# New constants in the planner that orders the work of a linear-attention and MoE kernel

## The chip, the cores and the metric

One core of one Trainium2 chip. The metric is the device time of one execution in microseconds; the number quoted is the median of three executions.

## The reference

Two parts, one after the other (cut to what is computed):

```python
mag = np.sqrt(a_re * a_re + a_im * a_im)
scale = np.minimum(mag, 0.999) / (mag + 1e-06)
ar, ai = a_re * scale, a_im * scale              # B=4, H=8, S=768, D=48
for t in range(S):
    new_re = ar[t] * S_re - ai[t] * S_im         # the state: D x D for each (b, h)
    new_im = ar[t] * S_im + ai[t] * S_re
    S_re, S_im = new_re + k[t] v[t]^T, new_im
    y[t] = q[t] @ S_re
x = y reordered to 3072 tokens x 384
h = x @ w_in                                     # 384 -> 2048
out = (gelu_erf(h)) @ w_out                      # 2048 -> 384
```

The weights arrive as float64 words; the result is float32.

## The kernel before, in words

The kernel has four kinds of work, and each step of each kind carries its kind's name.

- **lanes0 to lanes3** (`ticks`, `tick`, L1091, L703): the running products of the decays, on 128 partitions, in 24 slices of 8 rows over four groups of the sequence. For a slice s: `normalise` (part a: squares, `Ln`/`Exp` on ACT, multiplications of tiles `a` and `tab`), `scan` (part s: for each row one DVE product `tt` and one DVE sum `bt`), `towards` and `against` (part b: products into `xt`, then DMAs of `xt` to DRAM `kq`). `ending` (part e) closes a group.
- **weights** (`weights`, w0 to w15, each an "in" and an "out" piece): the float64 words of a piece are loaded into `raw`, ACT squares them for a range flag, four DVE steps build `wh` and the low half (`wi_lo`/`wo_lo`), ACT copies the high half (`wi_hi`/`wo_hi`), three PE products with `ident_r` and `minus` sum what the high half left over, and a copy (ACT or DVE) stores it as low half.
- **units** (`unit`, u0 to u23, 128 tokens each): loads `kqn` and `vn`, turns them (by PE transposes up to u7, by DVE transposes from u8), scores `qT,kp`, the state `st` with its gain (`m`), and the output, split into `xT` high (ACT) and `xT` low (DVE).
- **blocks** (`block`, j0 to j8, 2 or 3 units each): for each of 16 slices f of the hidden width, `first(f)` multiplies `xT` with `wi_hi`/`wi_lo` into `ph`; ACT writes `gh` and `gf` (Gelu), DVE `gl` = `gf` − `gh`; `second(f)` multiplies `gh` with `wo_hi` and `wo_lo`, and `gl` with `wo_hi`, into `po`. The units of the next block are written between the slices f of this one.

None of this is issued in the order of the code. `Plan` records every call as a step with its engine (or several engines that could run it, `either` and `both`), its cost from a table of constants, and what it depends on. `natural` (L274) gives each step a rank: the longest path to the end, plus an offset for the step's kind, `MORE`. The vector steps of the lanes are a chain of their own: along it each step counts with `WL` times its cost. `forward` (L292) plays the program through with a model of the queues; at every moment an engine takes the ready step with the highest rank, and a step that several engines can run goes where its modelled end plus `BIAS` of that engine is smallest. `backward` takes the ranks anew from the result; after four such passes (`PASSES`) the shortest modelled order is kept and issued (`issue`, L420 ff., hence all instructions carry L429). On the chip each engine, and SP's DMA queue, runs its instructions strictly in that order.

The few lines that use the three constants:

```python
if s.chain is not None:
    if s.chain in nextof:
        t = max(t, rest[nextof[s.chain]] + cost * s.weight)
...
return [t + MORE[s.kind] for t, s in zip(rest, steps)]
...
ends = {o: max(free[o], ready[i], ...) + c + BIAS[o] for o, (_, c) in steps[i].options.items()}
if ends[e] > min(ends.values()) + 1e-9:
    ...
...
P.chain["vector"] = "lanes", WL
```

Of the kernel before, what the change touches and what calls it, by code (L numbers as in the profile page):

```python
# [94 lines left out]
EARLIER, N_RAW, N_KP = 1, 4, 2  # L95
PASSES = 4
N_A = 4
WL = 4.532

MORE = dict(lanes0=483.83, lanes1=-1595.06, lanes2=-3639.85, lanes3=-3453.18, weights=-1624.01, units=-66.21, blocks=-85.66)  # L100
BIAS = dict(vector=-0.82, scalar=-1.94, gpsimd=0.93, sync=-6.23)


class Step:
# [8 lines left out]
class Plan:  # L113
# [160 lines left out]
    def natural(self):  # L274
# [4 lines left out]
        for i in range(len(steps) - 1, -1, -1):  # L279
# [9 lines left out]
            rest[i] = t  # L289
        return [t + MORE[s.kind] for t, s in zip(rest, steps)]  # L290

    def forward(self, rank):  # L292
# [14 lines left out]
        while len(order) < len(steps):  # L307
            best = None
            for e, waiting in pool.items():
# [8 lines left out]
                if len(steps[i].options) > 1:  # L318
                    ends = {o: max(free[o], ready[i], port[other[o]] if o in steps[i].port else 0.0) + c + BIAS[o] for o, (_, c) in steps[i].options.items()}
                    if ends[e] > min(ends.values()) + 1e-9:  # L320
# [119 lines left out]
def lanes_and_chunks(ctx, tc, flags, a_lanes, x_lanes, v_units, w_in, w_out, out):  # L440
# [650 lines left out]
    def ticks(g):  # L1091
        P.chain["vector"] = "lanes", WL
        with P.work(f"lanes{g}"):
            for s in range(end):
                if slices[s][0] == g:
                    tick(s)
        P.chain.pop("vector")
# [255 lines left out]
```

## Time and profile before

| | us |
|---|---|
| executions | 660.78, 662.86, 663.88 |
| median | 662.86 |
| span of the profiled execution, first to last instruction | 659.6 |
| median less that span | 3.3 |
| PE busy (share of the span) | 614.1 (93%) |
| DVE busy | 484.1 (73%) |
| ACT busy | 434.1 (66%) |
| POOL busy | 26.1 (4%) |

The profile is of one execution and gives its span only; times of single steps are times of that execution. PE is TensorE, PEld its weight loads, DVE VectorE, ACT ScalarE, POOL GpSimd, SP the queue of the DMAs. Names such as `gl<-gf,gh` are the tile written and the tiles read, as the program names them. A row of a timeline begins with the start in us from the start of the span and the duration.

### The profile page before, as it was taken

The numbers are of one execution on the slowest core, as the hardware profiler recorded it, in microseconds if no ns is written. First come the engines' busy times: TensorE is split into PE (matmuls) and PEld (weight loads), VectorE is DVE, ScalarE is ACT, GpSimd is POOL, SyncE is SP. The second block draws the span as 40 slices with busy tenths as digits, with TensorE's granted clock in tenths as the row PEclk, the third lists the DMA queues.
The fourth block names the chain that finished last, engine by engine and source line by source line (L and its number), as shares of the span: only waits on it lengthen the run. The fifth ranks groups of instructions, "written<-read, shape, count | busy, mean of one in ns | idle before, by whom it ended". The sixth has DMA issues, their size and how long they took to land.

```text
span 659.6 us, 13997 instructions
## 1 busy us (share of the span) xinstructions
PE 614.1 (93%) x5154; PEld 563.8 (85%) x5154; DVE 484.1 (73%) x1204; ACT 434.1 (66%) x1107; POOL 26.1 (4%) x74
## 2 busy tenths in 40 slices
PE   4655499999999999999999999999999999999995
PEld 2322277988789999999999999999999999999995
DVE  6999999999999999999989999656334424232211
ACT  8976699999998979787476997535442422232332
POOL 1000100002000000120000000020000000000000
PEclk9787699999999999999999999999999999999999
DMA  9366876668266456687889966487444132110000
GB/s 322 119 158 161 256 225 212 185 196 258 71 197 173 116 135 177 163 173 158 198 198 219 230 157 166 116 167 169 104 88 88 50 64 46 34 51 15 25 1 27
DMA packets 210442, 93.51 MB, mean 142 GB/s; under 512 B 167744, under 2 KB 202688, under 8 KB 210368
## 3 DMA queue, kind: packets, MB, share of 16 engines
q1 hardware_dynamic: 210368, 92.57, 54.6%
q8 instruction: 41, 0.67, 0.4%
q14 instruction: 33, 0.27, 0.1%
HBM read 63.11 MB, written 25.69 MB: 135 GB/s over the span
## 4 chain that ended last, share of the span: by engine, by line
PE 70%; ACT 9%; DVE 9%; issue 2%; DMA 1%; SPq 0%; DVEq 0%; ACTq 0%
PE po L429 27%; PE ph L429 26%; PE att L429 17%; DVE a L429 2%; ACT a L429 1%; DVE tt L429 1%; ACT tab L429 1%; ACT L429 1%; ACT L427 1%; DVE xt L429 1%; ACT gh L429 1%; DVE bt L429 1%; ACT gf L429 1%; DMA raw<-in_w_pieces_dram 1%; ACT square L429 1%
## 5 line engine op out<-in xcount | busy, mean ns | idle before, releaser
L429 PE MATMUL ph<-xT,wi_hi 128*128 128x384 f32 (+1 forms) x864 | 209.2, 324 | 0.0
L429 DVE TENSOR_TENSOR gl<-gf,gh 128x384 fp32r<-128x384 f32 (+1 forms) x144 | 73.7, 512 | 126.4 <-ACT gf L429 126.0
L429 ACT ACTIVATE gh<-ph 128x384 fp32r<-128x384 f32 (+1 forms) x144 | 65.8, 457 | 149.6 <-PE ph L429 149.2
L429 PEld LDWEIGHTS ph<-xT,wi_hi 128*128 128x128 f32 x864 | 154.3, 188 | 2.2 <-ACT gf L429 0.2
L429 PE MATMUL ph<-xT,wi_lo 128*128 128x384 f32 (+1 forms) x432 | 137.3, 318 | 0.0
L429 PE MATMUL po<-wo_hi,gh 128*128 128x384 f32 x384 | 132.5, 345 | 0.9 <-ACT gh L429 0.7
L429 PE MATMUL po<-wo_lo,gh 128*128 128x384 f32 x384 | 129.7, 338 | 0.0
L429 PE MATMUL po<-wo_hi,gl 128*128 128x384 f32 x384 | 92.5, 342 | 0.0
L429 PEld LDWEIGHTS ph<-xT,wi_lo 128*128 128x128 f32 x432 | 81.3, 188 | 0.1
L429 PEld LDWEIGHTS po<-wo_hi,gh 128*128 128x128 f32 x384 | 72.1, 188 | 3.0 <-ACT gh L429 2.0
L429 PEld LDWEIGHTS po<-wo_lo,gh 128*128 128x128 f32 x384 | 72.5, 189 | 0.0
L429 DVE TENSOR_TENSOR tt<-bt,a 128x192 f32<-128x192 f32 x192 | 67.3, 350 | 0.5
L429 PEld LDWEIGHTS po<-wo_hi,gl 128*128 128x128 f32 x384 | 65.9, 188 | 1.6 <-DVE gl L429 0.7
L429 ACT ACTIVATE gf<-ph 128x384 f32<-128x384 f32 (+1 forms) x144 | 65.4, 454 | 2.5 <-DVE gl L429 2.5
L429 DVE TENSOR_TENSOR bt<-tt 128x96 f32<-128x96 f32 x192 | 48.1, 250 | 0.5
L429 PEld LDWEIGHTS att<-qT,kp 96*64 96x64 f32 (+1 forms) x512 | 39.4, 165 | 2.4 <-issue 1.5
L429 PE MATMUL att<-qT,kp 96*64 96x64 f32 (+1 forms) x512 | 41.0, 250 | 0.0
L429 DVE TENSOR_TENSOR kp<-att,causal 128x512 f32<-128x512 f32 x40 | 27.5, 687 | 9.5 <-PE att L429 9.4
L429 ACT ACTIVATE a<-tab 128x384 f32<-128x384 f32 (+1 forms) x48 | 25.6, 534 | 9.3 <-DVE tab L429 9.2
L429 PE MATMUL po<-wh,ident_r 128*128 128x384 f32 x48 | 22.0, 541 | 9.4 <-DVE wh L429 9.3
L429 PE MATMUL att<-tab,ident_r 128*128 128x384 f32 (+1 forms) x20 | 14.8, 896 | 13.6 <-ACT tab L429 13.6
L429 ACT ACT_TABLE_LOAD x21 | 26.9, 1283 | 0.3
(154 smaller groups left out, 992.9 us busy)
## 6 DMA issues: line engine op xcount, KB each, us to landing
kqn<-kq SPq DMA_DIRECT2D x96, 128.0 KB, 3.2
xt<-in_x_lanes_dram SPq DMA_DIRECT2D x24, 384.0 KB, 4.4
kq<-xt SPq DMA_DIRECT2D x48, 192.0 KB, 3.5
a<-in_a_lanes_dram SPq DMA_DIRECT2D x20, 384.0 KB, 3.4
raw<-in_w_pieces_dram SPq DMA_DIRECT2D x16, 384.0 KB, 4.1
raw<-in_moe_w_out_dram SPq DMA_DIRECT2D x16, 384.0 KB, 4.3
vn<-in_v_units_dram SPq DMA_DIRECT2D x24, 256.0 KB, 3.7
kqn<-kq SPq DMA_DIRECT2D x8, 768.0 KB, 5.7
```

The lines of the kernel that those rows point to most:

```text
L427: self.nc.scalar.preload_act_table_set(table)
L429: getattr(getattr(self.nc, engine), name)(*args, **kw)
```

## The change

Three constants of the planner get other values: the weight of the lanes' chain on VectorE, the offsets of the kinds of work, and the bias by which a step that several engines can run chooses. The steps, their costs in the model and the passes are as they were.

```diff
--- before.py
+++ after.py
@@ -95,10 +95,10 @@
 EARLIER, N_RAW, N_KP = 1, 4, 2
 PASSES = 4
 N_A = 4
-WL = 4.532
-
-MORE = dict(lanes0=483.83, lanes1=-1595.06, lanes2=-3639.85, lanes3=-3453.18, weights=-1624.01, units=-66.21, blocks=-85.66)
-BIAS = dict(vector=-0.82, scalar=-1.94, gpsimd=0.93, sync=-6.23)
+WL = 13.504
+
+MORE = dict(lanes0=-1432.76, lanes1=-1644.43, lanes2=-1748.35, lanes3=-7390.72, weights=-1708.45, units=3080.11, blocks=24.45)
+BIAS = dict(vector=-1.99, scalar=-3.28, gpsimd=46.61, sync=-6.23)
 
 
 class Step:
```

The program issues the same steps; their order on each engine differs at many places, and some 40 steps (copies, multiplications by a constant or by a gain) run on ACT in place of DVE or the other way. One switch of ACT between the Gelu table and the Ln/Exp table and back is gone. Three places are shown, in the names of the rows (a number behind a name is that of the buffer).

On ACT, near 79 us of the trace before: the squares of a weight piece (`square<-raw`), the square of a lane's tile (`tab<-a`, 128x864) and the square of another lane's scan result (`a<-bt`). Before:

```order
L429 ACTIVATE square0_126,flags_58<-raw2_118 128x384
L429 ACTIVATE tab0_133<-a33_130 128x864
L429 ACTIVATE a30_127<-bt0_131 128x2x384
L429 CAST wo_hi_102<-wh1_125 128x384
L429 ACTIVATE square0_126,flags_58<-square0_126,by_partition_82 128x384
L429 CAST wi_lo_101<-po2_115 128x384
```

After the change:

```order
L429 ACTIVATE square0_126,flags_58<-raw2_118 128x384
L429 ACTIVATE a30_127<-bt0_131 128x2x384
L429 ACTIVATE square0_126,flags_58<-square0_126,by_partition_82 128x384
L429 CAST wo_hi_102<-wh1_125 128x384
L429 ACTIVATE tab0_133<-a33_130 128x864
L429 CAST wi_lo_101<-po2_115 128x384
```

The square of `bt0` stands ahead of the weight piece's second step and of `tab0<-a33`, which it followed.

On DVE, near 178 to 180 us of the trace before: the lower halves of unit u4's output (`xT1`, `x67`), the last steps of weight piece w15 (`wo_lo`), lanes (`tt`, `bt`, `a3..`, `tab`, `xt`), and the 15th `gl` of block j0. Before:

```order
L429 TENSOR_TENSOR xT1_154<-att2_110,xT1_154 128x3x64
L429 TENSOR_TENSOR tt0_134<-bt1_132,a31_128 128x192
L1274 TENSOR_SCALAR flags_58<-flags_58 128x32
L429 TENSOR_TENSOR x670_155<-att1_109,x670_155 128x64
L429 TENSOR_TENSOR xT1_154<-att1_109,xT1_154 128x3x64
L429 SCALAR_TENSOR_TENSOR wo_lo_103<-raw3_119 128x384
L429 TENSOR_TENSOR bt1_132<-tt0_134 128x2x48
L429 TENSOR_TENSOR a33_130<-tab0_133,a33_130 128x384
L429 TENSOR_TENSOR tt1_135<-bt1_132,a31_128 128x192
L429 SCALAR_TENSOR_TENSOR tab0_133<-a33_130,tab0_133 128x384
L429 TENSOR_TENSOR bt1_132<-tt1_135 128x2x48
L429 TENSOR_TENSOR gl0_164<-gf0_166,gh0_162 128x256
```

After the change:

```order
L429 TENSOR_TENSOR x670_155<-att1_109,x670_155 128x64
L429 TENSOR_TENSOR xT1_154<-att1_109,xT1_154 128x3x64
L429 TENSOR_TENSOR a30_127<-a30_127,xt0_136 128x384
L429 TENSOR_TENSOR bt1_132<-tt0_134 128x2x48
L429 TENSOR_TENSOR xt0_136<-a30_127,bt0_131 128x8x96
L429 SCALAR_TENSOR_TENSOR tab0_133<-tab0_133,a33_130 128x384
L429 TENSOR_TENSOR tt1_135<-bt1_132,a32_129 128x192
L429 SCALAR_TENSOR_TENSOR a33_130<-a33_130,by_partition_82,tab0_133 128x384
L429 TENSOR_TENSOR bt0_131<-tt1_135 128x2x48
L429 TENSOR_TENSOR a33_130<-a33_130,tab0_133 128x384
L429 TENSOR_TENSOR tt0_134<-bt0_131,a32_129 128x192
L429 TENSOR_TENSOR gl0_164<-gf0_166,gh0_162 128x256
```

The last `xT1` has the w15 `wo_lo` and the lane steps that followed it before (two `bt`, two `tt`, two of `a33` and `tab0`) ahead of it now; between it and the `gl` stand nine lane steps of two slices, where there were six, one of them a `wo_lo`.

On PE, at the same time: transposes of unit u5 (`ident_r,kqn1`), its state product (`m20`) and scores (`qT`, `kp`), the last piece of w15 (`wh1`, `minus`), and block j0. Before:

```order
L429 MATMUL po2_115<-wh1_125,ident_r_80 128x384
L429 MATMUL po2_115<-wo_hi_102,minus_78 128x384
L429 MATMUL po2_115<-wo_lo_103,minus_78 128x384
L429 MATMUL att1_109<-ident_r_80,kqn1_145 96x128 x4
L429 MATMUL att2_110<-ident_r_80,kqn1_145 96x128 x4
L429 MATMUL po0_113<-wo_hi_102,gl0_164 128x384
L429 MATMUL po1_114<-wo_hi_102,gl0_164 128x384
L429 MATMUL po0_113<-wo_hi_102,gh1_163 128x384
L429 MATMUL po0_113<-wo_lo_103,gh1_163 128x384
L429 MATMUL att1_109<-m20_148,ident_r_80 128x384
L429 MATMUL att1_109<-m20_148,other_half_91 128x384
L429 MATMUL att0_108<-qT0_149,kp0_151 64x64 x8
```

After the change:

```order
L429 MATMUL att1_109<-ident_r_80,kqn1_145 96x128 x4
L429 MATMUL att2_110<-ident_r_80,kqn1_145 96x128 x4
L429 MATMUL ph1_112<-xT0_153,wi_hi_100 128x256 x2
L429 MATMUL ph1_112<-xT0_153,wi_lo_101 128x256
L429 MATMUL po1_114<-wo_hi_102,gh0_162 128x384
L429 MATMUL po1_114<-wo_lo_103,gh0_162 128x384
L429 MATMUL att1_109<-m20_148,ident_r_80 128x384
L429 MATMUL att1_109<-m20_148,other_half_91 128x384
L429 MATMUL att0_108<-qT0_149,kp0_151 64x64 x8
L429 MATMUL att0_108<-qT1_150,kp1_152 64x64 x8
L429 MATMUL po0_113<-wo_hi_102,gl0_164 128x384
L429 MATMUL po1_114<-wo_hi_102,gl0_164 128x384
```

The w15 piece has moved ahead of all of u5's transposes, and the `gl` products, which stood ahead of u5's `m20` and scores, now follow both.

## Rows read from the trace of the kernel before

**Rows 1.** Busy time, share of the span and instructions of each engine.

```profile
PE 614.1 (93%) x5154; PEld 563.8 (85%) x5154; DVE 484.1 (73%) x1204; ACT 434.1 (66%) x1107; POOL 26.1 (4%) x74
```

**Rows 2.** PE's busy share in 40 slices of 16.5 us, in tenths.

```profile
PE   4655499999999999999999999999999999999995
```

**Rows 3.** Windows: length, PE, PEld, DVE, ACT, POOL busy (instructions), clock, DMA share, GB/s.

```profile
40.00:60.00 20.00, 9.62 (x23) 4.79 (x22) 18.56 (x52) 13.21 (x31) 0.26 (x2) 0.83 0.62 160
60.00:84.00 24.00, 14.54 (x30) 7.21 (x29) 23.48 (x66) 15.76 (x37) 3.37 (x7) 0.64 0.88 254
84.00:110.00 26.00, 26.00 (x445) 20.57 (x444) 24.54 (x66) 25.85 (x79) 0.00 (x0) 1.00 0.71 209
110.00:140.00 30.00, 29.97 (x364) 26.42 (x360) 29.76 (x83) 29.82 (x73) 1.51 (x3) 1.00 0.61 181
140.00:185.00 45.00, 44.46 (x412) 36.66 (x412) 43.64 (x117) 44.75 (x122) 4.83 (x11) 1.00 0.58 175
185.00:260.00 75.00, 75.00 (x793) 71.19 (x793) 72.86 (x197) 64.03 (x147) 0.13 (x1) 1.00 0.59 156
480.00:650.00 170.00, 169.93 (x1218) 167.67 (x1217) 52.45 (x105) 54.05 (x158) 0.02 (x1) 1.00 0.20 45
```

**Rows 4.** Waits of PE, whole span: us in total, times, longest.

```profile
PE att L429 <- ACT tab L429: 13.6, 4, 4.9
```

**Rows 5.** Waits of DVE from 0 to 85 us.

```profile
DVE tab L429 <- ACT tab L429: 5.5, 2, 5.2
DVE a L429 <- ACT a L429: 2.5, 3, 1.5
DVE tab L429 <- ACT a L429: 0.5, 1, 0.5
```

**Rows 6.** Timeline of DVE, 177.9 to 182.7 us: start, duration, engine, line, operation.

```profile
177.91 0.55 DVE L429 SCALAR_TENSOR_TENSOR wo_lo<-raw 128x384 fp32r<-128x384 uint32 x1
178.37 0.25 DVE L429 TENSOR_TENSOR bt<-tt 128x96 f32<-128x96 f32 x1
...
179.74 0.26 DVE L429 TENSOR_TENSOR bt<-tt 128x96 f32<-128x96 f32 x1
179.91 0.42 DVE L429 TENSOR_TENSOR gl<-gf,gh 128x256 fp32r<-128x256 f32 x1
180.24 0.36 DVE L429 TENSOR_TENSOR tt<-bt,a 128x192 f32<-128x192 f32 x1
180.51 0.56 DVE L429 SCALAR_TENSOR_TENSOR tab<-tab,a 128x384 f32<-128x384 f32 x1
...
182.62 0.96 DVE L429 TENSOR_TENSOR xt<-a,bt 128x768 f32<-128x768 f32 x1
```

**Rows 7.** Timeline of PE, 178.9 to 183.9 us.

```profile
178.97 0.81 PE L429 MATMUL po<-wh,ident_r 128*128 128x384 f32 x2
...
179.96 0.70 PE L429 MATMUL att<-ident_r,kqn 128*96 128x128 f32 x8
...
180.91 0.34 PE L429 MATMUL po<-wo_hi,gh 128*128 128x384 f32 x1
...
181.30 0.91 PE L429 MATMUL att<-m,ident_r 96*128 96x384 f32 x2
...
183.87 0.44 PE L429 MATMUL po<-wo_hi,gh 128*128 128x384 f32 x1
```

**Rows 8.** Timeline of ACT, 78.9 to 79.8 us.

```profile
78.93 0.91 ACT L429 ACTIVATE tab<-a 128x864 f32<-128x864 f32 x1
79.75 0.83 ACT L429 ACTIVATE a<-bt 128x768 f32<-128x768 f32 x1
```

**Rows 9.** Timeline of PE, 80.6 to 84.8 us.

```profile
80.63 2.93 PE L429 MATMUL att<-a,ident_r 128*128 128x384 f32 x4 [1.74 <-ACT a L429]
...
84.80 0.38 PE L429 MATMUL ph<-vn,kqn 64*64 64x48 f32 x6
```

**Rows 10.** ACT's table loads among the groups of the page.

```profile
L429 ACT ACT_TABLE_LOAD x21 | 26.9, 1283 | 0.3
```

## The prediction

> **What bounds the kernel now.** I read the page's totals first. PE is busy for 93% of the span and DVE for 73% [rows 1]. A total mixes stages, so the slices come next: PE's digits stand at 4 to 6 for the first five slices (16.5 us each, to about 82 us) and at 9 from there to the end [rows 2]. The windows tell what limits each stage [rows 3]. Between 40 and 84 us DVE is busy 42.04 of 44 us and PE only 24.16: VectorE sets the pace, with the first lanes and the splitting of the first weights. From 84 to 185 us PE is busy 100.43 of 101 us, but DVE (97.94) and ACT (100.42) are full too, so PE's busy time need not be useful work here. From 185 us on PE has 75.00 of 75 us, later 169.93 of 170, while DVE falls to 52.45 of 170. From there to the last product the time is PE's own work, and no order shortens it. An order can only gain in what stands ahead of 185 us, and it can lose anywhere by making PE wait.
>
> What PE waits for in the first stage is seen in its waits: the longest sum is for ACT's `tab` [rows 4]. DVE's own waits up to 85 us are for ACT: 2.5 us for `a`, 0.5 us for `tab` behind ACT's `a`, and 5.5 us for `tab`, 5.2 of it the kernel's start, which no order of later steps removes [rows 5]. So 3.3 us of it can be had.
>
> **The change, part by part.** No step is added or removed; the constants choose ranks and engines. The predicted time is the median of before, 662.86 us, plus the terms below; the span of the profiled execution, from which all durations come, is 659.6 us, 3.3 us under that median, and I take the same distance for the changed kernel.
>
> *Term 1, the end of the crowded stage, +1.0 us.* PE is solid from here on, so its end moves with the moment at which DVE has delivered u4's last `xT` and block j0's last `gl`, less whatever PE has already done by then. In the DVE excerpt, seven steps come ahead of the last `xT` that stood behind it: the w15 `wo_lo`, two `bt`, two `tt` and two multiplications of `a` and `tab`. In the trace these seven run right behind it: from the start of `wo_lo` to the start of the step after the second `tt` is 180.51 − 177.91 = 2.60 us, less the 0.33 us that `gl` takes in between (179.91 to 180.24), so 2.27 us [rows 6]. Two copies of 128 by 384 (the w13 `wo_lo`, u4's `st`) go to ACT; the nearest row, `wo_lo` to the next start, is 0.46 us with what follows it, so −0.92. `xT` comes 1.35 us later, if DVE is never idle. On PE u5's first transposes have one w15 piece more ahead of them (about 1.0 us: 178.97 to 179.96 [rows 7]) and two block pieces fewer (a gh piece from 180.91 to 181.30 is 0.39 us; I take 0.35 each). PE has thus done 0.3 us more by then: 1.35 − 0.3 = +1.05. For `gl` ten steps come ahead that were behind: three `tt` (0.36), two `bt` (0.26), one `xt` (0.96) and four of the kind of 0.56 [rows 6], 4.80 us; rows start 0.08 to 0.09 us before the one ahead has ended (177.91 + 0.55 against the next at about 178.37), so some 4.0 us, less the two copies: +3.1. On PE u5's `m` and `qT,kp` products now come ahead of that `gl`, 183.87 − 181.30 = 2.57 us in the trace [rows 7]: +0.5 against before. The two delays lie one behind the other and the later one holds: +1.0. Below it the term is 0 (the later steps are hidden in DVE's 3.1 us of idle time between 84 and 185 us [rows 3]), above it +3.1 (PE's moved steps wait for DVE themselves and fill nothing).
>
> *Term 2, idle time of DVE ahead of that point, −2.5 us.* DVE has 1.44 + 0.52 + 1.46 + 0.24 + 1.36 = 5.0 us idle between 40 and 185 us [rows 3]. The change could take all of it or none. It speaks for a gain that ACT now runs what a lane waits for earlier: at 78.9 us the trace has `tab` (0.91 us) ahead of the square of `bt` (0.83 us) [rows 8], and PE waits 1.74 us for that square, which feeds four products of 2.93 us together [rows 9], in a window of a mean granted clock of 0.64 against 1.00 in the next [rows 3]. In the ACT excerpt the two have changed places, so PE's products can start up to 0.8 us sooner. DVE also has three rows fewer ahead of the end of that scan. Against it: lanes0 first means fewer weight steps, which fill DVE while a lane waits for ACT. Neither end can be excluded, so I take the middle.
>
> *Term 3, one pair of table loads fewer, 0.* Lanes a7 and e7 now share one Ln/Exp set between the Gelus, so two loads go, 1.283 us each by the mean of 21 [rows 10], 2.57 us of ACT. ACT is full from 84 to 185 us, and the saving lies there; but the two copies of term 1 and other moved steps come to ACT, and what PE waits on last is DVE. If ACT were last it would be −2.57, which I keep inside the range. The Trainium skill (ScalarE: Activation LUTs, What ACT_TABLE_LOAD costs) gives about 1283 ns for a load and some 1380 ns of draining beside it, 2.66 us for a switch. The trace agrees on the load; by the page the pair would be worth some 5.3 us of ACT, an estimate that enters no sum.
>
> *Term 4, everything behind 185 us, 0.* Units u13, u14 and u18 to u23 come earlier on PE, but it is full either way. Near 290 us unit u8's products have six block pieces fewer ahead; a piece is three products, and the 1218 of 480 to 650 us take 0.14 us each [rows 3], so PE is there 2.5 us sooner, while DVE's list ahead of u8's keys is only about 0.9 us shorter. If that wait is not covered by u8's slack it costs up to +1.6 us.
>
> Sum: +1.0 − 2.5 + 0 + 0 = −1.5, and 662.86 − 1.5 = 661.4 us (span 658.1). A measurement of this kernel can tell a difference of 0.5%, 3.3 us, from none: faster is under 659.5, slower over 666.2. The forecast is no difference that can be told, with its own range from 659.5 to 666.
>
> **The rivals.** *Faster: the crowded stage opens.* PE's busy rows from 84 to 185 us say that no room is left. The weight loads in the same windows say otherwise: 20.57 + 26.42 + 36.66 = 83.65 of 101 us, against 71.19 of 75 (95%) from 185 to 260 [rows 3]. At 95% the same loads take 88.1 us, 12.9 less: products are being held in the pipeline by other engines. If weights w9 to w13, which come 6 to 14 us of DVE work earlier, feed j0 in time, all 5.0 us of DVE's idle time go and term 1 stands: 662.86 − 5.0 + 1.0 = 658.9. If half of the 12.9 us goes, it is 656.4. Against it: DVE is 97% busy there and its steps are the same in number, so only its idle time can be had, unless lanes are pushed behind 185 us, and the excerpt shows the opposite. Chance 0.37. The Trainium skill (Perfetto Trace Analysis, Identifying the Most-Contended Engine) says that busy matmuls are no measure of headroom and that weight-load busy time is; by that rule the 12.9 us are the ceiling of this rival, and the rows above bear it out as far as the load share differs between the stages.
>
> *Slower: PE's order has run ahead of DVE's.* At j0's end and at u8 PE now arrives sooner than DVE's work allows. If u5's `m` and `qT,kp` fill nothing, because they wait on DVE as well, the first costs 3.1 us, the second 1.6 us, and with no idle time gained ahead: 662.86 + 4.7 = 667.6. It speaks for it that DVE has 72.86 of 75 us from 185 to 260 [rows 3], so a delay there is not made up quickly. Against it: until 185 us PE has work of three kinds to choose from. It decides from the point at which term 1 and u8 together cost more than 3.3 us over what term 2 brings. Chance 0.22.
>
> *It does nothing that can be seen*, since only the span ahead of 185 us is open: that is the forecast, chance 0.41.
>
> **How the numbers follow.** Faster by over 0.5%: 0.37. Same: 0.41. Slower: 0.22. The range takes the faster rival to between its two figures and the pair of table loads beyond it (655.5), and the slower one to its full price (667.5). That leaves about 2 in 10 outside.
>
> **What would show it.** Right: DVE's idle time from 40 to 185 us falls to about 2.5 us; unit 0's first product, at 84.80 us before [rows 9], starts about 1 us earlier; the last `gl` of j0 is on DVE at 180 to 182 us; PE shows no wait over 0.5 us after 185. The faster rival shows weight-load busy time over 85% between 84 and 185 us. The slower one shows waits of PE on DVE's `xT`, `kp` or `gl` of over 3 us together after 140 us. The forecast is wrong if PE's solid stretch begins later than 86 us, or ends more than 3 us away from 651.

## The result, and the profile after

The changed kernel takes 667.39 us by the median of 17 executions (663.09 to 670.32), the kernel before 662.52 us by the median of 17 (659.82 to 667.63); the ratio is 1.0059, with a 95% interval from 1.0034 to 1.0084. In a second series it was 1.0052 (1.0025 to 1.0080). The ratio is taken over all executions and not from the two medians, which lie 4.9 us apart in the first series and 3.8 us in the second; by it the change makes the kernel slower by some 0.55%, 3.7 us. Ratios here compare executions in the fast state alone; one of head_again below, 670.26 us, was in the slow one. The forecast was 661.4 us, "no difference that can be told", so it was wrong: the time lies outside the forecast's own range (659.5 to 666) and just inside the wider one that takes in the rivals (655.5 to 667.5), and it moved to the other side, just past the bound of 0.5%, to the figure of the slower rival.

The profiled execution of the changed kernel took 664.72 us with a span of 662.9 us. The page's totals and PE's slices, which answer to [rows 1, 2]:

```profile
PE 613.7 (93%) x5154; PEld 563.7 (85%) x5154; DVE 483.8 (73%) x1200; ACT 438.3 (66%) x1124; POOL 21.8 (3%) x73
...
PE   4465799998999999999999999999999999999995
```

The totals say nothing: PE has the same work to within 0.4 us. The slices do. PE's digits reach 9 at the same place as before, but behind it stands one 8 where before no slice fell under 9. The windows that answer to [rows 3] (length, PE, PEld, DVE, ACT, POOL busy with their instructions, clock, DMA share, GB/s):

```profile
40.00:60.00 20.00, 11.46 (x24) 6.25 (x24) 19.76 (x57) 14.39 (x35) 0.47 (x3) 0.74 0.72 194
60.00:84.00 24.00, 15.97 (x95) 9.80 (x95) 23.36 (x65) 19.21 (x47) 3.38 (x7) 0.72 0.88 265
84.00:110.00 26.00, 24.88 (x393) 19.15 (x392) 24.89 (x67) 24.63 (x79) 0.00 (x0) 1.00 0.55 165
110.00:140.00 30.00, 29.06 (x345) 25.04 (x345) 29.57 (x80) 29.62 (x80) 1.21 (x3) 1.00 0.66 198
140.00:185.00 45.00, 41.56 (x406) 35.30 (x404) 41.86 (x118) 41.58 (x105) 4.02 (x11) 1.00 0.58 170
185.00:260.00 75.00, 74.50 (x787) 69.85 (x787) 72.47 (x192) 64.91 (x153) 0.26 (x2) 1.00 0.60 161
```

Up to 84 us everything is better: PE has 27.43 us of work where it had 24.16, and DVE is idle for 0.24 + 0.64 = 0.88 us in place of 1.96. From 84 to 185 us everything is worse: PE is busy 95.50 of 101 us (100.43 before), its weight loads 79.49 (83.65), and DVE is idle for 4.68 us (3.06). The three largest sums of PE's waits from 84 us on (us in total, times, longest), of which before had 0.7 us for `gh` and none of the other two kinds:

```profile
PE po L429 <- ACT gh L429: 2.4, 3, 1.9
PE ph L429 <- DMA xT<-x: 1.2, 1, 1.2
PE att L429 <- DVE kp L429: 0.9, 1, 0.9
```

To see where time is lost, each step of PE was given a price: the lower quartile, over all steps of the same shape in the two traces, of the time from its start to the start of PE's next step. What a stretch takes beyond the prices of its steps is lost there, waits and stretched products alike. In us:

```
stretch          before   changed   changed less before
0 to 85 us        49.1      44.7         -4.4
85 to 110          2.5       4.3         +1.8
110 to 140         2.1       3.4         +1.4
140 to 185         4.6       6.6         +2.0
185 to 260         2.3       3.4         +1.1
260 to the end     9.0       9.2         +0.2
```

The sum, +2.1, is what PE's last product comes later (654.02 us against 651.98). The prices are those of this study, and the borders of the stretches are moments at which the two orders have not done the same work. Three steps that both orders have make a sharper cut: unit 0's first product (84.80 us before [rows 9], 80.50 after), block j1's first, and the last product of all. Before, the last two of these are

```profile
184.32 0.52 PE L429 MATMUL ph<-xT,wi_hi 128*128 128x384 f32 x2
651.98 0.55 PE L429 MATMUL po<-wo_hi,gl 128*128 128x384 f32 x2
```

and after the change 184.26 us (its row stands with the third wait below) and

```profile
654.02 0.55 PE L429 MATMUL po<-wo_hi,gl 128*128 128x384 f32 x2
```

```
from, to                       before   changed   changed less before
start, unit 0                    84.8      80.5         -4.3
unit 0, block j1                 99.5     103.8         +4.2
block j1, the last product      467.7     469.8         +2.1
```

In this pair of traces the start and the crowded stage cancel, and what is left lies behind j1. These 2.1 us are not chance: from j1's first product to the last one all eight traces with the changed order in that part took 469.7 or 469.8 us, and all five with before's order there 467.6 or 467.7. Some 0.4 us of it shows as idle time of PE; 1.2 us of it lies in block j1. The rest of the difference of 3.3 us between the two spans lies behind the last instruction that does work: 7.2 us to the end of the span against 5.9. Over the eighteen traces of this study that stretch was 5.5 to 8.3 us long, without regard to the order, so it is not put down to the change.

### The profile page after: what moved, and what is told of

Read it like the earlier page. It is cut to its first block, busy times and chain, and to the rows that moved or that the text cites. A ratio compares the mean times of both kernels' runs of the same rounds, so it can differ in the third digit from the quotient of the medians.

```text
span 662.9 us, 14031 instructions
## 1 busy us (share of the span) xinstructions
PE 613.7 (93%) x5154; PEld 563.7 (85%) x5154; DVE 483.8 (73%) x1200; ACT 438.3 (66%) x1124; POOL 21.8 (3%) x73
## 4 chain that ended last, share of the span: by engine, by line
PE 70%; ACT 12%; DVE 9%; DMA 5%; issue 3%; SPq 1%; DVEq 0%; ACTq 0%
PE po L429 27%; PE ph L429 26%; PE att L429 16%; ACT tab L429 2%; ACT a L429 2%; DVE a L429 2%; ACT square L429 2%; DMA raw<-in_w_pieces_dram 2%; ACT L427 1%; ACT L429 1%; DVE tt L429 1%; DMA xT<-x 1%; DVE wh L429 1%; ACT gh L429 1%; SPq L429 1%
## 5 line engine op out<-in xcount | busy, mean ns | idle before, releaser
L429 PE MATMUL po<-wo_hi,gh 128*128 128x384 f32 x384 | 134.0, 349 | 2.8 <-ACT gh L429 2.4
L429 PE MATMUL att<-tab,ident_r 128*128 128x384 f32 (+1 forms) x20 | 12.3, 756 | 18.9 <-ACT tab L429 18.9
L429 PEld LDWEIGHTS att<-kp,vn 128*64 128x64 f32 (+1 forms) x448 | 20.2, 135 | 7.6 <-issue 4.5
```

The costliest lines, as they stand in the source:

```text
L429: getattr(getattr(self.nc, engine), name)(*args, **kw)
```

## The experiments

Three theories stood at the beginning. **A**: the first 80 us of the new order gain 4 to 5 us, and its order from 84 to 185 us gives them away again. **B**: DVE and ACT are full up to 185 us, so an earlier unit 0 is eaten by waits whatever order follows. **C**: an early unit 0 meets TensorE at half clock in most executions.

**One order up to a point, the other from there.** The planner makes both orders; the merged one takes the first so many steps of each engine from one of them, and all that are left in the order (and on the engines) of the other. Any such pair keeps every dependency, since both are complete orders of the same steps.

```diff
+FIRST = dict(WL=13.504, MORE=..., BIAS=...)
+THEN = dict(WL=4.532, MORE=..., BIAS=...)
+CUT = {'vector': 203, 'scalar': 106, 'gpsimd': 11, 'tensor': 25, 'sync': 48}
...
+        left, merged = dict(CUT), []
+        for i in plans[0][2]:
+            e = plans[0][1][i][0]
+            if left[e]:
+                left[e] -= 1
+                merged.append((i, plans[0][1][i]))
+        done = {i for i, _ in merged}
+        merged += [(i, plans[1][1][i]) for i in plans[1][2] if i not in done]
```

This is the first of them, the new order up to unit 0 and before's from there:

> The changed order up to unit 0's first transpose (79.9 us in its trace), before's order and engines for all steps that are left then. Theory A (the first 80 us of the new order gain 4 to 5 us, its order between 84 and 185 us gives them away again): about 658.5, ratio 0.992 to 0.996. Theory B (DVE and ACT are full up to 185 us, so an earlier unit 0 is eaten by waits whatever order follows): 661 to 664, ratio 0.998 to 1.002. Theory C (an early unit 0 meets TensorE at half clock in most executions): 664 to 667, ratio over 1.003.

660.05 us against 664.09, ratio 0.9941 (0.9918 to 0.9964). In a later series the same kernel was measured again:

> The changed order up to unit 0, before's order from there, once more on this chip, as the measure for the next run: ratio 0.992 to 0.997.

660.04 us against 662.36, ratio 0.9963 (0.9944 to 0.9983). Theory B and theory C fall: the early start is worth 2.3 to 4 us when before's order follows it, and it is faster than both kernels. The windows of the second of these traces:

```profile
40.00:60.00 20.00, 12.41 (x28) 6.71 (x26) 19.70 (x55) 15.56 (x37) 0.26 (x2) 0.75 0.72 193
60.00:84.00 24.00, 14.99 (x70) 8.65 (x70) 23.93 (x67) 18.06 (x43) 3.66 (x7) 0.71 0.89 252
84.00:110.00 26.00, 25.86 (x420) 20.52 (x420) 25.22 (x67) 25.28 (x78) 0.00 (x0) 1.00 0.69 201
110.00:140.00 30.00, 30.00 (x357) 26.89 (x355) 29.17 (x81) 29.82 (x76) 1.64 (x4) 1.00 0.63 180
140.00:185.00 45.00, 44.45 (x456) 36.21 (x456) 43.46 (x118) 44.34 (x115) 4.68 (x10) 1.00 0.62 181
```

The first two are as good as the changed kernel's (DVE idle for 0.37 us); behind 84 us the waits of the changed kernel are absent, with PE busy 100.31 of 101 us and its weight loads at 83.62, before's figures. From unit 0 to j1 the two traces took 101.6 and 100.3 us. The early start itself is seen in every trace: with the new first steps unit 0's first product starts at 79.9 to 83.2 us (eleven traces), with before's at 84.8 to 86.9 (four).

The other way round, `FIRST` with before's constants up to unit 0's first product, `THEN` with the new ones:

> Before's order up to unit 0's first product (84.8 us in its trace), the changed order for all that is left. Theory A: the new order between 84 and 185 us costs its 5 us and the part behind 185 us 1 to 3 more, with no early start against it: 668 to 671, ratio 1.008 to 1.012. Theory B: 662 to 665, ratio 1.000 to 1.004. Theory C (only the early start is dear): 661 to 664.

673.26 us against 664.09, ratio 1.0127 (1.0092 to 1.0161): theory A, a little over its range. And the new order only behind 185 us:

> Before's order up to block j1's first product (184.3 us), the changed order from there. If the part behind 185 us costs what the two traces show (1.7 us more of small waits there, 0.4 given back behind 480, 1.3 us more from the last copy to the end of the span): 664 to 665.5, ratio 1.002 to 1.005. If these are chance: 662.5, ratio 0.999 to 1.001.

667.84 us, ratio 1.0059 (1.0037 to 1.0080), above what was expected. From j1's first product to the last its trace took 470.3 us, where before's order took 467.7 and the changed kernel 469.8. So 2.1 of these 2.6 us are what the order behind j1 costs in every trace, and some 0.5 belong to the join, where PE waits once for unit u5's `m`:

```profile
PE att L446 <- DVE m L446: 1.1, 1, 1.1
```

At a join, the steps that the new order had done earlier come first, ahead of what PE needs next. In that trace unit 0 also started 2.1 us later than in before's, with the same order up to there. The crowded stage was then tried by itself, with a second cut that returns to before's order at block j1:

> Before's order up to unit 0's first product, the changed order from there to block j1's first product, before's order for all that is left: the crowded stage of the change by itself, the prediction's term 1. If the parts add up (head_new 0.9941, after185_new 1.0059, tail_new 1.0127): 1.0127 - 0.0059 = 1.0068, some 4.5 us. If the part behind 185 us cost only because it followed a late start: 1.010 or more. If term 1 was right and the rest is chance: 1.0015.

670.65 us against 662.36, ratio 1.0116 (1.0092 to 1.0140). That is the second of the expectations by its number, but not by its reason. The parts do not add up in the way expected; the crowded stage alone costs nearly what the whole rest of the order costs (1.0127). By these two ratios the order behind 185 us adds 0.1%, with intervals of some 0.3% on either; by the traces, which are far more alike, it adds 2.1 us (467.7 in this kernel, 469.7 in the one before it), 0.3%, behind a late start as behind an early one. The stage from unit 0 to j1 took 107.4 us in both, against 99.5 before. Its windows:

```profile
84.00:110.00 26.00, 26.00 (x377) 19.64 (x375) 23.36 (x66) 24.57 (x77) 0.00 (x0) 0.98 0.66 206
110.00:140.00 30.00, 27.77 (x340) 24.11 (x337) 26.93 (x76) 27.06 (x75) 0.82 (x3) 0.89 0.60 181
140.00:185.00 45.00, 42.55 (x400) 36.87 (x400) 40.79 (x108) 40.62 (x102) 4.00 (x11) 0.96 0.50 149
```

PE is busy 96.32 of 101 us, DVE is idle for 9.92 us, and the clock is below full in all three windows of the stage: it falls to half for 6.8 us from 112.3 and for 3.4 us from 167.0. This was the slowest of the six executions (672.36 us). The 7.9 us that the stage is longer here are thus the order and the clock together; without a fall of the clock the same stage costs 4.2 us in the changed kernel. PE's largest waits are two of the changed kernel's; the third cannot occur, since j1 follows before's order:

```profile
PE po L454 <- ACT gh L454: 3.0, 3, 1.9
PE att L454 <- DVE kp L454: 0.9, 1, 0.9
```

So theory A is right as far as it goes: the start gains 4.3 us, and the stage up to j1 gives 4.2 away where the clock stays up, more where it falls. The 2.1 us behind j1 are not in it.

**Which wait, and is each paid?** In the six traces of the changed kernel three of PE's waits stand at the same steps, the first two in all six (0.86 us, and 1.7 to 1.9), the third in five (0.65 to 1.2; not in trace4). First, u2's scores are followed directly by the product that needs the `kp` made from them, with nothing of another kind between:

```profile
104.73 1.46 PE L429 MATMUL att<-qT,kp 96*64 96x64 f32 x32
107.06 0.62 PE L429 MATMUL att<-kp,vn 64*64 64x64 f32 x14 [0.86 <-DVE kp L429]
```

The `kp` on DVE begins 0.12 us after the scores have ended; it is not late, PE has just come to it too soon. Second, late in block j0, ACT does the logarithm of lane a8 ahead of a `gh` that PE waits for:

```profile
152.29 0.84 ACT L429 ACTIVATE tab<-a 128x768 f32<-128x768 f32 x1
153.02 0.54 ACT L429 ACTIVATE square<-raw 128x384 bf16<-128x384 f32 x1
...
153.56 0.51 ACT L429 ACTIVATE a<-a 128x384 f32<-128x384 f32 x1
154.09 1.28 ACT L427 ACT_TABLE_LOAD   x1
155.38 0.62 ACT L429 ACTIVATE tab<-tab,by_partition 128x384 f32<-128x384 f32 x1
156.04 0.53 ACT L429 ACTIVATE tab<-tab 128x384 f32<-128x384 f32 x1
156.58 1.28 ACT L429 ACT_TABLE_LOAD   x1
157.88 0.38 ACT L429 ACTIVATE gh<-ph 128x256 fp32r<-128x256 f32 x1
```

From 152.29 to 157.88 us stand 5.6 us of steps of lanes and of w15, two table loads among them. PE, meanwhile:

```profile
155.75 0.69 PE L429 MATMUL att<-ident_r,kqn 128*96 128x128 f32 x8
158.31 0.45 PE L429 MATMUL po<-wo_hi,gh 128*128 128x384 f32 x1 [1.87 <-ACT gh L429]
```

Third, block j1's first product waits for the transfers of u4's `xT`, which in SP's queue are behind unit u6's 768 KB:

```profile
182.49 0.62 PE L429 MATMUL po<-wo_hi,gl 128*128 128x384 f32 x2
184.26 0.59 PE L429 MATMUL ph<-xT,wi_hi 128*128 128x384 f32 x2 [1.15 <-DMA xT<-x]
```

Before's first product of j1 came at 184.32 us, with the same transfers landing between 183.2 and 184.1: it did not wait, since PE had u5's scores and a `gh` to do until then [rows 7]. In the next kernel six steps of the new order are moved, to take the second and third wait out:

```diff
+MOVES = [
+    ((913, 914), 'before', 957),
+    ((1347, 1348), 'before', 1354),
+    ((1484, 1485), 'after', 1337),
+]
```

(913 and 914 are j0's `gh` and `gf`, 957 the logarithm; 1347 and 1348 j0's last `gh` products, 1354 j1's first; 1484 and 1485 the loads of u6, 1337 the last `xT` transfer of u4.)

> The changed order with three waits of PE taken out by moving eleven lines of its list and nothing else: j0's `gh` and `gf` ahead of lane a8's Ln/Exp with its two table loads on ACT (PE waited 2.0 us there in the new order's traces), j0's second `gh` products ahead of j1's first product on PE, and u6's loads behind u4's `xT` transfers in SP's queue (together 1.2 to 1.4 us). Theory A (these waits are the cost, each is paid): 2 to 3.5 us less than the changed kernel, ratio to before 0.999 to 1.003. Theory B (DVE and ACT set the pace to 185 us, a wait taken out shows again further on): ratio 1.004 to 1.007, and the trace shows the waits of 155 and 184 us gone but others grown by as much.

665.55 us against 662.84, ratio 1.0049 (1.0021 to 1.0077): by the number theory B, but the interval reaches into theory A's range, and the ratio cannot be told from the changed kernel's 1.0052 to 1.0059. The trace is clearer than the times. Its clock falls at the same places as in the first trace of the changed kernel (nowhere between 80 and 650 us), and against that one the last work ends 1.8 us sooner; of the 3.3 us of waits between 140 and 200 us, 1.5 are left, at other steps:

```profile
PE att L451 <- ACT qT L451: 0.8, 1, 0.8
PE po L451 <- ACT gh L451: 0.7, 1, 0.7
```

So about half of what the moves removed was paid for and half came back at other steps, by this one pair of traces.

**The constants one at a time.** Only the units' offset new, only that offset old, and only the bias new:

```diff
-MORE = dict(lanes0=483.83, ..., units=-66.21, blocks=-85.66)
+MORE = dict(lanes0=483.83, ..., units=3080.11, blocks=-85.66)
```

> Before's constants, only the units' offset new (-66 to 3080): PE takes a unit's step as soon as it is ready by the model. Its PE order is as near to the changed kernel's as the full change (1.2 places a step on average, 4.4 from before's). Theory D (units ahead of everything on PE are what costs behind 84 us): ratio 1.008 to 1.014, as with the changed order behind before's first 84 us. If the offset of the units is not the cause: 0.998 to 1.004.

> The changed constants, only the units' offset old. Theory D: the waits behind 84 us stay away and the early start remains: ratio 0.990 to 0.998. Rival: its DVE list ahead of u2 and u4 is 13 to 15 us longer than in either kernel (lane steps first), so DVE is late for the units: ratio over 1.005.

> Before's constants, only the bias of the engines new: PE's order stays before's (0.7 places a step), 27 steps run on another engine. If the engine choice gives the early start: unit 0 starts at 80 to 82 us and the ratio is 0.992 to 0.997. If the choice of engine is what costs behind 84 us: ratio over 1.004. If neither: 0.998 to 1.002.

Measured: 683.34 us, ratio 1.0321 (1.0289 to 1.0354); 695.10 us, 1.0482 (1.0446 to 1.0517); 668.58 us, 1.0099 (1.0063 to 1.0136). All three are slower than both kernels. The first went the way of theory D, but by more than twice its range; the second went against it, and over the rival's bound: taking that offset back makes the kernel slower still. So theory D (units ahead of everything are the cause) is not borne out. PE's longest wait in the second trace is for DVE, 3.8 us for a unit's `m`, as the rival had it, but 2.9 us for a transfer stand beside it, and the clock is at half for 24 us from 182; its 32 us were not traced further. The third, by its own expectation (over 1.004), says that the choice of engine alone can cost as much as the change. Its unit 0 starts at 83.1 us, not at 80 to 82, and PE's longest wait behind it is one of 2.9 us for the transfers of `xT` at j0's first product, which neither kernel has. The constants work as a set; undoing one of them does not undo a part of the change, it makes a third order with waits of its own. That is why the cuts above, which keep either order as it is, tell more.

**The clock.** The six traces of the unaltered changed kernel (two with the series, four single ones) were compared by when the granted clock stood at half:

> The changed kernel unaltered, for a second profile. If its time is the order's alone, the trace shows again a unit 0 that starts near 80 us, 5 us ahead of before, and 3 to 7 us more of PE waiting between 84 and 185 us; ratio 1.004 to 1.008. If it is the clock's, the trace of a slower execution shows TensorE at half clock past the start of unit 0, and its span is longer by about half of that stretch (up to 3.4 us).

> The changed kernel, one more traced execution. Clock theory: where the clock falls to half between 100 and 125 us the execution takes 667 us or more, where it doesn't 663 to 666. Rival: times and falls don't go together.

> The changed kernel, one more traced execution, with the same expectation: a fall of the clock between 100 and 125 us goes with 667 us or more, none with 663 to 666; by the rival they don't go together.

> The changed kernel, one more traced execution, with the same expectation: a fall of the clock between 100 and 125 us goes with 667 us or more, none with 663 to 666; by the rival they don't go together.

> The changed kernel, one more traced execution, with the same expectation: a fall of the clock between 100 and 125 us goes with 667 us or more, none with 663 to 666; by the rival they don't go together.

```
trace    time us   half clock behind 85 us         unit 0   unit 0 to j1   j1 to the last
first    664.72    none                              80.5      103.8          469.8
trace3   664.62    none                              80.6      103.8          469.7
trace4   665.01    3.4 us from 107.9                 79.9      104.7          469.7
again    669.24    6.8 us from 109.0                 82.8      106.7          469.7
trace5   669.56    6.8 us from 109.3                 83.2      106.7          469.7
trace6   671.87    6.8 from 109.5, 3.4 from 164.1    83.2      108.1          469.7
before   (span 659.6)  none                          84.8       99.5          467.7
```

Five of the six go with the clock theory, and trace4 does not: its clock fell in the stretch named, and it took 665.01 us where 667 or more was expected. Nor is the fall the whole difference. The order is the same in all six, so the same step can be compared: at 108 us, ahead of the fall, again, trace5 and trace6 were already 1.9 to 2.3 us behind the first trace, and 1.2 to 2.5 us behind it at 19 us. What makes such a start slower was not looked for. A fall of 6.8 us (to the lower of the two levels, 1.2 GHz) then adds 2.9 us to the stage, a second one of 3.4 us another 1.4. In trace4 the 3.4 us at half clock set the steps back by 1.5 us, and most of it came back at j1's first product, which in the first trace waits for u4's transfers and in trace4 does not. (The execution of before beside trace3 to trace6 took 665.07 us, but it is a single one.) Of the 29 executions of the two series eleven took 663.1 to 666.2 us and eighteen 667.1 to 673.5; which of those without a trace had a fall is not known. The windows of trace5, and the middle one of trace3, where the clock stays up:

```profile
100.00:109.00 9.00, 8.43 (x140) 6.52 (x139) 8.40 (x24) 8.62 (x31) 0.00 (x0) 1.00 0.73 238
109.00:116.00 7.00, 6.71 (x59) 5.72 (x60) 5.79 (x15) 5.09 (x16) 0.00 (x0) 0.52 0.56 168
116.00:125.00 9.00, 8.20 (x103) 6.93 (x102) 8.36 (x26) 8.16 (x23) 0.00 (x0) 0.99 0.76 246
```

```profile
109.00:116.00 7.00, 7.00 (x90) 5.62 (x89) 7.00 (x20) 7.00 (x23) 0.00 (x0) 1.00 0.94 300
```

The fall comes right behind the wait for u2's `kp`, and the products that follow take nearly twice their time (the w10 piece 1.65 + 1.09 us in place of some 0.9 + 0.6):

```profile
107.07 1.36 PE L429 MATMUL att<-qT,kp 96*64 96x64 f32 x32
109.29 1.11 PE L429 MATMUL att<-kp,vn 64*64 64x64 f32 x16 [0.86 <-DVE kp L429]
...
112.01 1.65 PE L429 MATMUL po<-wh,ident_r 128*128 128x384 f32 x2
```

The fall that the first expectation had in mind, at the start of unit 0, was not there: in that trace (again) the clock is full from 81.6 us to the fall at 109.0, and unit 0's transposes start at 82.2. A fall between 100 and 125 us was seen in four of the six traces of the changed kernel, in both kernels with this crowded stage behind before's start, in only_bias and in units_old; not in three_moves and units_new, and in none of the five traces with before's order in that stage. What brings it about was tried with products that nothing needs, put into two of PE's gaps:

```diff
+FILL = {(795, 0): 4, (764, 0): 4}
...
+                for _ in range(FILL.get((number[id(s)], n), 0)):
+                    self.nc.tensor.matmul(**self.fill)
```

> The changed order with eight products that nothing needs (128x128x128, four ahead of u2's `kp,vn` products, four ahead of j0's first `gh` products), in the two gaps of PE ahead of 110 and of 118 us. Clock theory (in about half of the executions the granted clock falls to half behind the first of these gaps, as in the second trace at 109.0 us, and that costs 3 us): no half-clock stretch between 90 and 190 us, times between 663 and 666, median 1.5 to 2.5 us under the changed kernel's, ratio 1.001 to 1.004. Rival (the clock falls for another reason, or costs nothing that DVE does not cost): ratio 1.005 to 1.007 and times up to 670 as before.

669.93 us against 662.36, ratio 1.0098 (1.0061 to 1.0135), over the range of either theory. The clock fell all the same, for 10.2 us from 106.6, and the products overran their gap: the step before u2's `kp,vn` lost 3.1 us in place of 1.2. The clock theory's prescription failed; that a gap of PE is what makes the clock fall is not shown, and what does stays open. The same in the first 80 us of the kernel with the new start:

> As head_again, with 53 products that nothing needs in six gaps of PE between 30 and 74 us (70% of each gap). Clock theory: the granted clock stays full for most of 30 to 80 us (mean over 0.9 against 0.6 to 0.8), unit 0 never meets half clock, and PE's sums of the lanes' squares take half as long: 0.5 to 2 us less than head_again. If DVE alone sets the pace up to 80 us: the clock rises and the time is that of head_again within 0.5 us. If the added products hold up those behind them in PE's queue: longer.

660.08 us, ratio 0.9968 (0.9946 to 0.9989), as head_again (0.9963). The mean clock of its executions lies between 0.976 and 0.985, that of head_again's between 0.968 and 0.972. It rose less than was expected; the windows from 30 to 80 us, head_again's first, and the only wait of DVE in that stretch with the products in:

```profile
30.00:80.00 50.00, 29.39 (x59) 15.75 (x60) 49.70 (x138) 37.71 (x88) 3.92 (x9) 0.70 0.73 195
30.00:80.00 50.00, 37.88 (x165) 28.09 (x164) 48.54 (x135) 36.71 (x86) 3.85 (x9) 0.81 0.70 191
```

```profile
DVE a L453 <- ACT a L453: 1.4, 1, 1.4
```

The clock rose from 0.70 to 0.81, and the time did not move. But DVE, which waited 0.2 us in this stretch in head_again, now waits 1.4, so the products may also have held something up, as the third expectation had it; the run does not separate the two. What head_again's window does show is that DVE is busy for 49.70 of the 50 us: it sets the pace there.

## Why the prediction was wrong

**What bounds the kernel** was read rightly as far as it goes: nothing behind 185 us shortened. But it grew, by the 2.1 us behind j1, and term 4 had 0 for that.

**Term 1 failed**: "The two delays lie one behind the other and the later one holds: +1.0." (By its own working the later delay is +0.5; +1.0 is the larger.) From unit 0 to j1 the changed kernel takes 103.8 us in place of 99.5, +4.2, where the clock stays up, and 106.7 to 108.1 where it falls for 6.8 us or more; the stage by itself, in mid_new, costs 1.16% (0.92 to 1.40), some 7.7 us, with falls in it. At the point that the term was worked out at, the two terms together had the end of the stage 1.5 us sooner. It did not move: u4's last `xT` and j0's last-but-one `gl` (the rows that answer to [rows 6]) are on DVE at 177.50 and 181.44 us where they were at 177.64 and 179.91, and j1 begins at 184.26 us where it began at 184.32.

```profile
177.50 0.35 DVE L429 TENSOR_TENSOR xT<-att,xT 128x192 fp32r<-128x192 f32 x1
...
178.40 0.95 DVE L429 TENSOR_TENSOR xt<-a,bt 128x768 f32<-128x768 f32 x1
...
181.44 0.42 DVE L429 TENSOR_TENSOR gl<-gf,gh 128x256 fp32r<-128x256 f32 x1
```

But unit 0 had begun 4.3 us earlier. That the end of the stage did not move at all means that the stage took that much longer, and the places where PE is seen to wait are those that the term did not look at: u2's `kp` (0.86 us), j0's first `gh` (0.26, and 0.8 where the clock had fallen), the `gh` behind a lane's logarithm (1.87), j1's `xT` (1.15). The term priced the end of the stage on two engines and took all else in the 100 us as unchanged, where PE's list had been put into another order throughout. In part of the executions the fall of the clock comes on top. What each of the waits is worth by itself was not settled: the one try, three_moves, could not be told from the changed kernel by its times.

**Term 2 was right in sign, and near in size, but not by its working.** With before's order behind it the early start is worth 2.3 to 4 us (0.9963 and 0.9941), so −2.5 would have stood. Unit 0 was said to start about 1 us earlier; it started 4.3 us earlier in the first trace and 1.6 to 4.9 in the six. The mechanism was seen at the place named: the square of `bt` runs ahead of `tab` on ACT, and at 74.94 us in place of 79.75 [rows 8]:

```profile
74.94 0.84 ACT L429 ACTIVATE a<-bt 128x768 f32<-128x768 f32 x1 [0.32 <-DVE bt L429]
...
76.69 0.92 ACT L429 ACTIVATE tab<-a 128x864 f32<-128x864 f32 x1
```

Unit 0's first products on PE, which answer to [rows 9]:

```profile
79.88 0.69 PE L429 MATMUL att<-ident_r,kqn 128*96 128x128 f32 x8
80.50 1.14 PE L429 MATMUL ph<-vn,kqn 64*64 64x48 f32 x32
```

The step to "all of DVE's idle time between 40 and 185 us, one half" failed, however: it fell from 1.96 to 0.88 us up to 84 us, as said, and rose from 3.06 to 4.68 from there, 5.56 in all where 2.5 was forecast. The idle time was not one pool; a start that comes sooner is an advantage only while the list behind it has work ready at that moment.

**Term 3** set the pair of table loads at 0 and kept a gain in the range. The page has 20 and 19 loads where it had one more each, and no gain from that is seen: between 84 and 185 us ACT is idle for 5.2 us where it was for 0.6. The shared set is at 131.06 to 137.05 us, where before had two sets between 129.62 and 139.46. PE's wait of 1.87 us stands behind a later set (lane a8's); before has one at the same place (154.25 to 160.27 us), and PE waited 0.47 us behind it. What the saved pair is worth was not tested. The Trainium skill's 2.66 us for a switch (ScalarE: Activation LUTs, What ACT_TABLE_LOAD costs) is not what the row shows: from the start of the load to the start of the next ACTIVATE there are 1.29 us (154.09 to 155.38).

**Term 4 failed too.** It looked at u8, and there the changed kernel has no wait; but 0 for "everything behind 185 us" is not what the order costs. From j1's first product to the last it takes 2.1 us more in every trace, wherever the part ahead comes from. That PE "is full either way" was taken from its busy time, which is nearly the same in both (75.00 and 74.50 of 75 us up to 260) and does not show it.

**The rivals.** The slower one gave 667.6 us and 667.39 was measured, and that the figures agree is luck: its sum had no idle time gained ahead, where the start gained 4.3 us, and 1.6 us at u8, which does not wait. Its mechanism, PE's order run ahead of those that feed it, is seen, but not at its places: j0's end waits for a transfer, and ACT holds PE up more often than DVE. Its condition was the right one to watch, what the start brings against what the stage behind it loses. It had 0.22 because the prediction took the stage's busy engines for a reason that little could change there, when an order that idles three full engines (PE by 4.9 us more, ACT by 4.6, DVE by 1.6) was the thing to fear. The faster rival had the opposite in view: the weight loads' share from 84 to 185 us did move, but down, from 83.65 to 79.49 us, and PE's busy time with it, from 100.43 to 95.50. The Trainium skill (Perfetto Trace Analysis, Identifying the Most-Contended Engine) judges headroom by the weight loads and not by the busy matmuls; here both show the loss, and with before's order behind the new start both are back (83.62 and 100.31).

## What to carry to other kernels

A list order gains and loses in different stages at once, and a sum over the places that one happens to compare misses the rest. Measure each stage between steps that both orders have, and not between moments; that is what brought out the 2.1 us behind j1. Then go through the whole stage and ask, for each product of the bound engine that follows directly on one it depends on, what stands between. Where two orders of the same steps are at hand, cut them together at the seams of the stages; here that gave a kernel of 660.05 us (0.9941 and 0.9963), faster than both, from parts of each. A join has a price of its own, so a cut is to be tried from both sides.

## What the runs showed of the hardware that was not expected

The granted clock can fall to half in the middle of a stage in which PE is busy for 95% of the time, in stretches that these traces show as 3.4 to 10.2 us long, in some executions of a program and not in others. A fall of 6.8 us made the stage 2.9 us longer; one of 3.4 us cost 0.9 to 1.4. Of six traces of one program the three with the longer fall took 669.2 to 671.9 us and the other three 664.6 to 665.0, but the former had been some 2 us late before it. A few unneeded products in two of the gaps did not prevent the fall in the one trace taken.

Where nothing of this kind interferes, the same order repeats closely: from block j1's first product to the last one, 470 us, thirteen traces of kernels with other parts ahead fall into two groups 2.1 us apart, by the order in that part, and within a group they agree to 0.2 us.
